# Two more places for expert weights, contiguous output pieces, and a reordered end of the main loop in a fused attention and mixture-of-experts kernel

## The chip, the cores and the metric

The kernel runs on one core of one Trainium2 chip. The metric is the device time of one execution in microseconds (us), as the median of several runs. The engines are PE (TensorE, with its weight loads shown apart as PEld), DVE (VectorE), ACT (ScalarE), POOL (GpSimd) and SP (SyncE). In this kernel SP computes nothing; it issues every transfer between DRAM and the on-chip memory, in one queue and in program order.

## What is computed

The reference is a chain of three parts, in fp32, on 8 batches of 576 tokens (4608 tokens in all):

```python
# 1. attention with 32 learned memories per head (8 heads of 64)
a = softmax(phi)                          # over 32 memories
k_m, v_m = a^T k, a^T v
attn = softmax(q k_m^T / 8) v_m
x = attn, heads side by side              # 4608 x 512
# 2. a maxout layer
h = max(x @ w1, x @ w2, x @ w3)           # 4608 x 768
x = h @ w_out                             # 4608 x 512
# 3. a soft mixture of 8 experts with 4 slots each
logits = x @ phi2                         # 4608 x 32
d = softmax(logits, over all tokens)
slot_input = d^T x                        # 32 x 512
slot_out[e] = relu(slot_input[e] @ e_w1[e]) @ e_w2[e]    # 512 -> 1024 -> 512
c = softmax(logits, over the 32 slots)
out = c @ slot_out                        # 4608 x 512
```

The softmax over all tokens splits the kernel in two: the experts can begin only when the last token's logits are known, and every output row needs all experts.

## The kernel before, in words

**The main part.** `ORDER` is a text of some 1,490 steps, written out one by one; each step is a short function (`ops`, L822), and the order of the text is the order of the instructions on every engine. `mn u hf r` (L585) makes six main products of unit u, half hf, of the r-th of the three maxout weights, into one of three `ps_m` banks; `ev u hf r` (L599) empties the bank: for r = 0 ACT copies it, for r = 1 and 2 DVE takes the maximum, the last of them into the h block `ht`. A unit is a batch n and one of six h blocks i; unit 47 is batch 7, block 5. `ht` is a ring of four buffers (L605), so block 5 of a batch takes the buffer of block 1. `trm`/`trc` (L635, L647) turn an h block: for batches 0, 1 and 7 on PE with a copy by ACT, for the others with a transpose on DVE, a write to DRAM (L645) and a read back (L663), both issued by SP. `lg` (L684) adds the logits of a block, into the single `ps_l` bank. `slm`/`sla` add the expert inputs of a batch into `s_run`. `hrc` copies the last 64 tokens of a block.

**The expert weights.** They are 64 pieces of 128 x 1024 fp32 (512 KB), used in the order input weights of expert 0, input weights of expert 1, first half of the output weights of expert 0, and so on, and at the end the second halves of all eight (L261 to L268). They are loaded into `NSLOT` = 41 places, many of them in memory that other data has left: piece k goes into place k modulo 41. `send(n)` (L278) issues the next n loads on SP. 32 of them are steps of `ORDER`; the others stand behind the main part (L847, L907, L935) and in the expert loops (L1019, L1037), always one `send` for each place's use. A load into a place waits until what was in it has been read, and whatever SP holds behind it waits too.

**The end.** From L848 on come the last block's logits and statistics, then the expert input (L911 to L946). The loop at L1044 runs, for each expert, `ex_in` (64 PE products for the hidden layer, ACT's relu), `ex_turn` (DVE) and `ex_out(e, 0)` (first 256 output columns, summed over experts in `acc[0]`). Then `so_a`, `so_b` bring the sum into two parts `sh` and `sl` for more exact products. The output is made in 9 groups r (eight of 4 x 128 tokens, and one of 8 x 64 tokens) by 2 halves x of 256 columns. `st_out(r, x)` (L1071) makes 12 products into four `ps_x` banks (all there are) and empties them with two copies by ACT and two by DVE into a free place. For r below `NH` = 6 each half goes out by itself, 512 KB in runs of 256 columns; for r = 6 to 8 the halves are put beside each other, and whole rows go out when the second half is made. The calls (L1110 to L1121) put `ex_out(r, 1)` and `st_out(r, 0)` in turns, then all of x = 1.

Of the kernel before, what the change touches and what calls it, by code (L numbers as in the profile page):

```python
# [7 lines left out]
FP32 = mybir.dt.float32  # L8
# [6 lines left out]
B, H, S, D, M = 8, 8, 576, 64, 32  # L15
DM, FF, E, F = 512, 768, 8, 1024
# [6 lines left out]
for _x in (2, 3, 4, 5, 12, 6, 7, 13, 8, 9, 14, 15, 10, 11):  # L23
    CV.append((768 * _x, 768))
NEG = -1.0e30
PIECE = 1024
NX = 6
# [131 lines left out]
)  # L159
W = [1, 0, 0, 3, 2]  # L160
LL = 0
VP = 3
EXTRA = 2
NSLOT = EXTRA + 9 + 12 + NX + 2 + 3 + 3 + 1 + 3


@with_exitstack
def kernel(
# [13 lines left out]
    nc = tc.nc  # L182
# [4 lines left out]
    ps_m = ctx.enter_context(tc.tile_pool(name="ps_m", bufs=3, space=PSUM))  # L187
    ps_l = ctx.enter_context(tc.tile_pool(name="ps_l", bufs=1, space=PSUM))
# [12 lines left out]
    def bank(pool, tag):  # L201
        return pool.tile([128, 512], FP32, tag=tag, name=tag)

    def mx():
        return bank(ps_x, "x")


    arena = keep.tile([128, (9 + 12 + NX) * PIECE], FP32, name="arena")
# [6 lines left out]
    s_run = keep.tile([128, FF], FP32, name="s_run")  # L215
    stat = keep.tile([128, 2], FP32, name="stat")
    h5x = keep.tile([128, 1920], FP32, name="h5x")
# [6 lines left out]
    hbuf = keep.tile([128, 3, 1536], FP32, name="hbuf")  # L224
# [17 lines left out]
    x0 = a0 + 12288  # L242
# [13 lines left out]
    slots = [extra[:, PIECE * j:PIECE * j + PIECE] for j in range(EXTRA)]  # L256
    slots += [arena[:, o:o + PIECE] for o in slot_off]
    late_slots = [h5x[:, 0:PIECE]] + [arena[:, PIECE * j:PIECE * j + PIECE] for j in range(9)]
    late_slots += [hbuf[:, 2, 0:PIECE], arena[:, x0:x0 + PIECE]]

    order = [("in", 0)]  # L261
    for e in range(E):
# [15 lines left out]
    def send(n):  # L278
        for _ in range(n):
            if sent[0] < len(pieces):  # L280
                x = slot(sent[0])
                if isinstance(x, list):
                    for g in range(4):
                        nc.sync.dma_start(out=x[g], in_=pieces[sent[0]][:, 256 * g:256 * g + 256])
                else:
                    nc.sync.dma_start(out=x, in_=pieces[sent[0]])
                sent[0] += 1
# [332 lines left out]
    lg = {}  # L620
# [186 lines left out]
    with tc.manual_schedule():  # L807
# [5 lines left out]
        def late_slots_in():  # L813
# [18 lines left out]
            slm=lambda n, k: sl_m(n, k, by_group(n, k)), sla=sl_a, mn=mn,  # L832
            send=send, rl=rest_logit, rx=lambda: st_exp(lg["r"], 96, 8), rtm=rest_tm, rtc=rest_tc,
# [4 lines left out]
        for x in ORDER.split(";"):  # L838
            x = x.split()
# [2 lines left out]

        main_x.close()
        more2 = ctx.enter_context(tc.tile_pool(name="more2", bufs=1, side="right"))
        more2_sb = more2.tile([128, 3 * PIECE], FP32, name="more2")
        slots.extend(more2_sb[:, PIECE * j:PIECE * j + PIECE] for j in range(3))
        send(3)  # L847
        L = B - 1  # L848
        st_logit(L, 5)
        last_logit(LL, 6)  # L850
        t = lg[L]
# [61 lines left out]
        for x in range(2):  # L913
            y = mx()
            for i in range(3):
                nc.tensor.matmul(
                    y[:, 32 * i:32 * i + 32], s_run[:, 128 * (3 * x + i):128 * (3 * x + i) + 128], wsel,
                    start=True, stop=True)
            if x:
                nc.vector.tensor_copy(out=st[x], in_=y[:, 0:96])  # L920
            else:
                nc.scalar.activation(out=st[x], in_=y[:, 0:96], func=ACTF.Copy)
        nc.vector.memset(msk, 0.0)
        warm(W[2], True)
        seen = set()
        for i in range(6):
            for c in ((1, 0) if i < 2 else (0, 1)):
                g = i if i < 4 else i - 4 + 2 * c
# [100 lines left out]
        def ex_out(e, x):  # L1029
            k0 = first["ab"[x], e]  # L1030
            for k in range(2):
                for g in range(4):
                    nc.tensor.matmul(  # L1033
                        acc[x][32 * g:32 * g + 32, 0:256], msk[:, e, k, g],
                        part_of(k0 + k, g),
                        start=(e == 0 and k == 0), stop=(e == E - 1 and k == 1), tile_position=(0, 32 * g))
                send(1)  # L1037
# [14 lines left out]
        def so_a(x):  # L1052
            nc.vector.tensor_copy(out=so_sb, in_=acc[x][:, 0:256])

        def so_b(x):
            t = mx()
            c = slice(256 * x, 256 * x + 256)
            nc.tensor.matmul(t[:, 0:256], sel, so_sb, start=True, stop=True)
            nc.scalar.activation(out=sh[:, c], in_=t[:, 0:256], func=ACTF.Copy)
            nc.vector.tensor_tensor(out=sl[:, c], in0=t[:, 0:256], in1=sh[:, c].bitcast(FP32), op=ALU.subtract)  # L1060

        ov = out.rearrange("(g x s) c -> x s g c", x=2, s=S)
        free = [slots[64 - NSLOT + j] for j in range(NSLOT - (64 - NSLOT))]
        free = [x for x in free if not isinstance(x, list)]

        NH = 6
        tok = {}
        for r in range(9):
            tok[r] = [free.pop(0) for _ in range(1 if r < NH else 2)]

        def st_out(r, x):  # L1071
            cs = slice(256 * x, 256 * x + 256)
            whole = r >= NH
            if not whole and x == 1 and free:
                tok[r] = [free.pop(0)]
            ts = [mx() for _ in range(4)]
            for k, (c, o) in enumerate(((ch, sh), (cl, sh), (ch, sl))):
                for g in range(4):
                    if r == 8 and g == 3:
                        continue  # L1080
                    rs = slice(32 * g, 32 * g + 32)
                    nc.tensor.matmul(  # L1082
                        ts[g][:, 0:256], c[rs, r], o[rs, cs], start=(k == 0), stop=(k == 2), tile_position=(32 * g, 0))
            if r == 8:
                for k, (c, o) in enumerate(((ch, sh), (cl, sh), (ch, sl))):
                    nc.tensor.matmul(ts[3][:, 0:256], c[:, 9], o[:, cs], start=(k == 0), stop=(k == 2))
            for g in range(4):
                if whole:
                    o = tok[r][g // 2].rearrange("p (g c) -> p g c", g=2)[:, g % 2, cs]
                else:  # L1090
                    o = tok[r][0].rearrange("p (g c) -> p g c", g=4)[:, g]
                if g % 2:
                    nc.vector.tensor_copy(out=o, in_=ts[g][:, 0:256])
                else:
                    nc.scalar.activation(out=o, in_=ts[g][:, 0:256], func=ACTF.Copy)
                if whole and x == 1 and g % 2:
                    o = tok[r][g // 2].rearrange("p (g c) -> p g c", g=2)
                    if r < 8:
                        nc.sync.dma_start(
                            out=out[S * r + 128 * g - 128:S * r + 128 * g + 128].rearrange("(g p) c -> p g c", p=128),  # L1100
                            in_=o)
                    else:
                        for y in range(2):
                            nc.sync.dma_start(out=ov[y, 512:576, g - 1:g + 1], in_=o[64 * y:64 * y + 64])
            if not whole:
                nc.sync.dma_start(
                    out=out[S * r:S * r + 512, cs].rearrange("(g p) c -> p g c", p=128),
                    in_=tok[r][0].rearrange("p (g c) -> p g c", g=4))

        so_a(0)  # L1110
        so_b(0)
        for r in range(9):
            if r < E:
                ex_out(r, 1)
            if r == E - 1:
                so_a(1)
            if r == E:
                so_b(1)
            st_out(r, 0)
        for r in [0, 1, 2, 3, 4, 5, 8, 6, 7]:  # L1120
            st_out(r, 1)  # L1121


# [57 lines left out]
```

## Time and profile before

| | us |
|---|---|
| median of 3 runs | 460.35 (460.18 to 460.82) |
| the profiled execution, its own time | 462.82 |
| its span, first to last instruction | 461.0 |
| PE busy in the span | 439.0 (95%) |
| DVE busy | 333.3 (72%) |
| ACT busy | 192.4 (42%) |
| POOL busy | 71.4 (15%) |

TensorE's granted clock is 0.976 of full speed in the mean. The transfers move 109.49 MB, 237 GB/s over the span. Times in all views count from the start of the span. "SPq" is SP's queue; a row of a transfer on it shows the issue, not the transfer. A landing is the time from the issue to the arrival of all data. In the views of stretches, the share is the mean busy share of the core's 16 DMA engines. In rows of instructions, the bracket gives the engine's idle time before the row and what ended it.

### The profile page before, as it was taken

The page shows a single profiled execution, that of the slowest core. Times are in us where ns is not written, and L with a number is a line of the kernel's source. Part 1 is how long each engine was busy: PE and PEld are TensorE (multiplying, and loading weights), DVE is VectorE, ACT ScalarE, POOL GpSimd, SP SyncE. Part 2 cuts the span into 40 slices and gives each one's busy share as a digit, 9 for nine tenths or more (in the row PEclk, how much of TensorE's full clock was granted, in tenths as well). Part 3 has the DMA queues.
Part 4 walks back from the last instruction along what each step waited for, and adds up shares of the span by engine and source line. Part 5 has one row for each costly group of instructions (what it writes and reads, how often), then busy time and mean ns, then how long its engine had stood idle before and what let it go on. Part 6 is the DMA issues. An engine that isn't in the chain of part 4 may idle for free.

```text
span 461.0 us, 12577 instructions
## 1 busy us (share of the span) xinstructions
PE 439.0 (95%) x5233; PEld 363.8 (79%) x5233; DVE 333.3 (72%) x753; ACT 192.4 (42%) x450; POOL 71.4 (15%) x92
## 2 busy tenths in 40 slices
PE   6989999999999999999999999999999999999982
PEld 5778889888887889978889698879878896654461
DVE  1596989879777986798769869899836444595441
ACT  2576766645524343334334334433433313233331
POOL 0235545620020011002100210030200000011000
PEclk9999999999999999999999999999999999999955
DMA  8987894217202395537468675388357775899988
GB/s 318 417 327 276 318 392 150 116 42 309 118 10 112 100 345 180 189 99 256 139 213 291 223 284 181 125 293 292 106 193 251 284 251 213 324 410 407 378 292 276
DMA packets 47657, 109.49 MB, mean 237 GB/s; under 512 B 3440, under 2 KB 26224, under 8 KB 45552
## 3 DMA queue, kind: packets, MB, share of 16 engines
q1 hardware_dynamic: 47600, 108.69, 65.2%
q8 instruction: 41, 0.67, 0.6%
q14 instruction: 16, 0.13, 0.1%
HBM read 91.38 MB, written 17.30 MB: 236 GB/s over the span
## 4 chain that ended last, share of the span: by engine, by line
PE 85%; DVE 5%; DMA 3%; issue 2%; ACT 2%; SPq 1%; POOL 1%; DVEq 0%; ACTq 0%; POOLq 0%
PE m L597 48%; PE x L564 7%; PE l L801 4%; PE x L439 3%; PE x L1082 3%; PE x L748 2%; DMA arena<-in_kv_dram 2%; PE x L475 2%; PE l L680 2%; PE m L1033 2%; PE m L1016 2%; PE x L639 2%; PE x L343 1%; PE l L1033 1%; SPq L663 1%
## 5 line engine op out<-in xcount | busy, mean ns | idle before, releaser
L597 PE MATMUL m<-ah,vh 128*128 128x288 f32 x576 | 171.4, 312 | 1.2 <-DVE ht L611 0.6
L597 PE MATMUL m<-ah,vl 128*128 128x288 f32 x576 | 161.8, 295 | 0.0
L597 PEld LDWEIGHTS m<-ah,vh 128*128 128x128 f32 x576 | 108.2, 188 | 20.6 <-issue 12.4
L597 PE MATMUL m<-al,vh 128*128 128x288 f32 x576 | 123.2, 295 | 0.1
L597 PEld LDWEIGHTS m<-ah,vl 128*128 128x128 f32 x576 | 108.4, 188 | 0.4
L597 PEld LDWEIGHTS m<-al,vh 128*128 128x128 f32 x576 | 92.3, 188 | 0.3 <-POOL al L532 0.3
L607 ACT ACTIVATE g<-m 128x288 f32<-128x288 f32 x96 | 38.9, 410 | 70.8 <-PE m L597 62.5
L609 DVE TENSOR_TENSOR g<-m,g 128x288 f32<-128x288 f32 x96 | 42.5, 449 | 31.0 <-PE m L597 24.4
L573 ACT ACTIVATE vh<-x 128x384 fp32r<-128x384 f32 (+1 forms) x100 | 42.0, 478 | 54.6 <-PE x L564 40.6
L611 DVE TENSOR_TENSOR ht<-m,g 128x288 f32<-128x288 f32 x96 | 42.4, 450 | 20.3 <-PE m L597 9.0
L579 DVE TENSOR_TENSOR vl<-x,vh 128x384 fp32r<-128x384 f32 (+1 forms) x100 | 48.7, 530 | 3.3 <-ACT vh L573 2.8
L564 PE MATMUL x<-arena,kvt 64*32 64x384 f32 (+1 forms) x800 | 39.5, 477 | 1.3 <-DVE vl L579 0.8
L532 POOL TENSOR_TENSOR al<-arena,ah 128x576 fp32r<-128x576 f32 x16 | 23.3, 1465 | 72.1 <-ACT ah L528 42.5
L325 POOL TENSOR_TENSOR arena<-arena 128x768 uint32<-128x768 uint32 (+1 forms) x13 | 23.5, 1808 | 34.5 <-ACT arena L313 24.2
L801 PE MATMUL l<-cst 128*128 128x128 f32 x162 | 25.0, 303 | 3.8 <-DMA cst<-in_consts_dram 3.2
L801 PEld LDWEIGHTS l<-cst 128*128 128x128 f32 x162 | 21.6, 208 | 7.1 <-DMA cst<-in_consts_dram 3.2
L616 POOL COPY arena<-ht 128x64 f32<-128x64 f32 x24 | 6.3, 279 | 124.5 <-DVE ht L611 98.9
L564 PEld LDWEIGHTS x<-arena,kvt 64*32 64x32 f32 x800 | 12.4, 105 | 13.5 <-issue 7.8
L439 PE MATMUL x<-arena 128*32 128x129 f32 x640 | 19.8, 274 | 1.1 <-DMA arena<-in_kv_dram 0.7
L643 DVE STREAM_TRANSPOSE arena<-ht 128x512 f32<-128x512 f32 x30 | 20.5, 697 | 0.2
L439 PEld LDWEIGHTS x<-arena 128*32 128x32 f32 x640 | 17.3, 110 | 3.2 <-DMA arena<-in_kv_dram 0.9
L481 DVE STREAM_TRANSPOSE arena<-x 128x288 f32<-128x288 f32 x32 | 13.3, 457 | 3.7 <-PE x L475 3.7
(246 smaller groups left out, 588.0 us busy)
## 6 DMA issues: line engine op xcount, KB each, us to landing
arena<-in_e_w_dram SPq DMA_DIRECT2D x44, 512.0 KB, 7.7
arena<-in_w_dram SPq DMA_DIRECT2D x14, 768.0 KB, 6.3
arena<-in_kv_dram SPq DMA_DIRECT2D x8, 1290.0 KB, 9.8
arena<-in_q_dram SPq DMA_DIRECT2D x16, 576.0 KB, 6.2
arena<-in_kv_dram SPq DMA_DIRECT2D x8, 1032.0 KB, 6.7
tr<-arena SPq DMA_DIRECT2D x30, 256.0 KB, 3.1
hbuf<-tr SPq DMA_DIRECT2D x30, 256.0 KB, 3.6
arena<-in_phi_t_dram SPq DMA_DIRECT2D x8, 576.0 KB, 5.9
```

The costliest lines, as they stand in the source:

```text
L325: (eng or nc.gpsimd).tensor_tensor(out=du, in0=du, in1=lo.bitcast(U32), op=ALU.add)
L439: nc.tensor.matmul(t[32 * g:32 * g + 32, 0:KVC], phin_sb[:, j, b, 32 * g:32 * g + 32], kv_sb[:, j, b, g] if j < 4 else kv4_sb[:, g], start ...
L532: nc.gpsimd.tensor_tensor(out=al[n][:, :, c], in0=aT_sb[:, :, c], in1=ah[n][:, :, c].bitcast(FP32), op=ALU.subtract)
L564: nc.tensor.matmul(t[b][32 * g:32 * g + 32, 128 * r0:128 * r1], kvt[n][r, b, 32 * g:32 * g + 32], w_sb[r, i, r0:r1, g], start=True, stop=T ...
L573: nc.scalar.activation(out=v1[n, i][0][:, b, c], in_=ph["v1", n, i][b][:, c], func=ACTF.Copy)
L579: nc.vector.tensor_tensor(out=vl[:, b, c], in0=ph["v1", n, i][b][:, c], in1=vh[:, b, c].bitcast(FP32), op=ALU.subtract)
L597: nc.tensor.matmul(t[:, 0:HALF], x, y, start=(k == 0), stop=(k == 5))
L607: nc.scalar.activation(out=g1[u, hf], in_=t[:, 0:HALF], func=ACTF.Copy)
L609: nc.vector.tensor_tensor(out=g1[u, hf], in0=t[:, 0:HALF], in1=g1[u, hf], op=ALU.max)
L611: nc.vector.tensor_tensor(out=ht[n, i][:, cs], in0=t[:, 0:HALF], in1=g1.pop((u, hf)), op=ALU.max)
L643: nc.vector.transpose(out=v, in_=ht[n, i][:, 0:512])
L801: nc.tensor.matmul(t[:, 0:128], ident, ident, start=True, stop=True)
```

## The change

Four things are changed.

1. `NSLOT` is 44. The pool `more2` holds five places, not three; a place made of `s_run[:, 512:768]` and three parts of `h5x` is added (its load is four transfers); the place in `hbuf` stands behind the `more2` places and not ahead of them. One `send` step fewer stands in `ORDER` (31), and the last of these stands behind the h read `trc 6 5`.
2. In `ORDER`, `trm 7 1; lg 7 1; trc 7 1` stand ahead of `mn 47 1 1; mn 47 1 2; mn 47 0 2` (18 main products); they stood behind. The last maxima `ev 47 0 2; ev 47 1 2` and `hrc 47` follow right behind the products.
3. The output tensor is laid out as 2 x 9 pieces of 128 x 1024, and each `st_out` writes one, contiguous, as soon as it is made. The host puts the rows in their order afterwards.
4. `ex_out(0, 1)` goes between `so_a(0)` and `so_b(0)`; six of the `st_out(r, 0)` are made before x = 1 is finished, and the other twelve calls use by turns the four `ps_x` banks and the three `ps_m` banks with `ps_l`. `so_b(1)` uses the `ps_l` bank.

```diff
@@ ORDER
-    "send 1; lg 7 0; mn 44 0 2; mn 44 0 0; ev 44 0 0; ev 44 1 1; ev 44 1 2; v1h 7 5; mn 44 0 1; ev 44 0 1; ev 44 "
-    "0 2; hrc 39; mn 45 1 0; mn 43 0 2; ev 45 1 0; mn 43 1 1; mn 45 0 0; ev 45 0 0; v1l 7 5; ev 43 0 2; hrc 44; "
-    "send 1; hrc 38; mn 43 1 2; ev 43 1 1; ev 43 1 2; hrc 43; mn 45 0 1; ev 45 0 1; trm 6 5; trc 6 5; mn 47 1 0; "
...
-    "2; mn 47 0 0; ev 47 0 0; mn 47 0 1; mn 46 1 1; mn 46 1 2; ev 46 1 1; ev 46 1 2; hrc 45; ev 47 0 1; mn 47 1 "
-    "1; hrc 46; mn 47 1 2; mn 47 0 2; ev 47 1 1; trm 7 2; trc 7 2; ltm 0 3; dtm 6; dtc 6; ev 47 0 2; trm 7 1; trc "
-    "6 3; trc 6 2; trm 7 4; trc 7 1; ev 47 1 2; trm 7 3; ltc 0 3; lg 7 1; slm 6 0; trc 7 3; slm 6 1; lg 7 2; lg 7 "
-    "3; trc 7 4; sla 6 0; sla 6 1; lg 7 4; hrc 47"
+    "lg 7 0; mn 44 0 2; mn 44 0 0; ev 44 0 0; ev 44 1 1; ev 44 1 2; v1h 7 5; mn 44 0 1; ev 44 0 1; ev 44 0 2; hrc "
+    "39; mn 45 1 0; mn 43 0 2; ev 45 1 0; mn 43 1 1; mn 45 0 0; ev 45 0 0; v1l 7 5; ev 43 0 2; hrc 44; hrc 38; mn "
+    "43 1 2; ev 43 1 1; ev 43 1 2; hrc 43; mn 45 0 1; ev 45 0 1; trm 6 5; trc 6 5; send 1; mn 47 1 0; v1h 7 4; "
...
+    "0 0; ev 47 0 0; mn 47 0 1; mn 46 1 1; mn 46 1 2; ev 46 1 1; ev 46 1 2; hrc 45; ev 47 0 1; trm 7 1; lg 7 1; "
+    "trc 7 1; mn 47 1 1; hrc 46; mn 47 1 2; mn 47 0 2; ev 47 1 1; ev 47 0 2; ev 47 1 2; hrc 47; trm 7 2; trc 7 2; "
+    "ltm 0 3; dtm 6; dtc 6; trc 6 3; trc 6 2; trm 7 4; trm 7 3; ltc 0 3; slm 6 0; trc 7 3; slm 6 1; lg 7 2; lg 7 "
+    "3; trc 7 4; sla 6 0; sla 6 1; lg 7 4"
 )
+NH = 4
-NSLOT = EXTRA + 9 + 12 + NX + 2 + 3 + 3 + 1 + 3
+NSLOT = EXTRA + 9 + 12 + NX + 2 + 3 + 5 + 2 + 3
...
-    late_slots += [hbuf[:, 2, 0:PIECE], arena[:, x0:x0 + PIECE]]
+    late_slots += [arena[:, x0:x0 + PIECE]]
...
-        more2_sb = more2.tile([128, 3 * PIECE], FP32, name="more2")
-        slots.extend(more2_sb[:, PIECE * j:PIECE * j + PIECE] for j in range(3))
-        send(3)
+        more2_sb = more2.tile([128, 5 * PIECE], FP32, name="more2")
+        slots.extend(more2_sb[:, PIECE * j:PIECE * j + PIECE] for j in range(5))
+        slots.append(hbuf[:, 2, 0:PIECE])
+        send(6)
...
+        slots.append([s_run[:, 512:768]] + [h5x[:, PIECE + 256 * j:PIECE + 256 * j + 256] for j in range(3)])
+        send(1)
         nc.vector.memset(msk, 0.0)
...
         def so_b(x):
-            t = mx()
+            t = bank(ps_l, "l") if x else mx()
...
-        def st_out(r, x):
+        def st_out(r, x, pool=None):
             cs = slice(256 * x, 256 * x + 256)
-            whole = r >= NH
-            if not whole and x == 1 and free:
-                tok[r] = [free.pop(0)]
-            ts = [mx() for _ in range(4)]
+            if pool:
+                ts = [bank(ps_m, "m") for _ in range(3)] + [bank(ps_l, "l")]
+            else:
+                ts = [mx() for _ in range(4)]
...
+            tok = free.pop(0)
             for g in range(4):
...
+                o = tok[:, 256 * g:256 * g + 256]
...
-            if not whole:
-                nc.sync.dma_start(
-                    out=out[S * r:S * r + 512, cs].rearrange("(g p) c -> p g c", p=128),
-                    in_=tok[r][0].rearrange("p (g c) -> p g c", g=4))
+            nc.sync.dma_start(out=out[x, r], in_=tok)
 
         so_a(0)
+        ex_out(0, 1)
         so_b(0)
-        for r in range(9):
-            if r < E:
-                ex_out(r, 1)
-            if r == E - 1:
-                so_a(1)
-            if r == E:
-                so_b(1)
-            st_out(r, 0)
-        for r in [0, 1, 2, 3, 4, 5, 8, 6, 7]:
-            st_out(r, 1)
+        for r in range(1, E):
+            ex_out(r, 1)
+            if r <= NH:
+                st_out(r - 1, 0)
+        so_a(1)
+        st_out(NH, 0)
+        so_b(1)
+        st_out(NH + 1, 0, True)
+        rest = [(r, 1) for r in range(9)] + [(r, 0) for r in range(NH + 2, 9)]
+        for i, (r, x) in enumerate(rest):
+            st_out(r, x, i % 2)
...
-    args.append(nc.dram_tensor("out_0_dram", (B * S, DM), _mybir.dt.float32, kind="ExternalOutput").ap())
+    args.append(nc.dram_tensor("out_0_dram", (2, 9, 128, 1024), _mybir.dt.float32, kind="ExternalOutput").ap())
```

## Rows read from the trace of the kernel before

**Rows 1.** The page, part 2: DMA busy tenths in 40 slices of the span.
```profile
DMA  8987894217202395537468675388357775899988
```

**Rows 2.** Timeline of SP's queue: start us, us of issuing, line, what, count.
```profile
366.75 1.41 SPq L286 DMA_DIRECT2D arena<-in_e_w_dram  x3
...
384.81 0.35 SPq L286 DMA_DIRECT2D hbuf<-in_e_w_dram  x1
...
385.73 1.35 SPq L286 DMA_DIRECT2D more<-in_e_w_dram  x3
...
394.07 1.28 SPq L286 DMA_DIRECT2D wo<-in_e_w_dram  x3
397.69 0.81 SPq L286 DMA_DIRECT2D extra<-in_e_w_dram  x2
398.59 17.77 SPq L286 DMA_DIRECT2D arena<-in_e_w_dram  x17
418.75 1.61 SPq L286 DMA_DIRECT2D more<-in_e_w_dram  x2
...
454.92 1.08 SPq L1099 DMA_DIRECT2D out_dram<-hbuf  x1
```

**Rows 3.** Stretches of the end: us, busy time of each engine, PEclk, DMA share, GB/s.
```profile
420.00:422.00 2.00, 2.00 (x30) 1.08 (x30) 0.42 (x1) 0.38 (x1) 0.46 (x1) 1.00 1.03 410
...
436.00:438.00 2.00, 1.55 (x15) 1.01 (x15) 0.98 (x4) 0.63 (x3) 0.00 (x0) 1.00 1.05 367
...
442.00:444.00 2.00, 1.73 (x19) 1.44 (x21) 0.76 (x2) 0.66 (x2) 0.00 (x0) 0.50 0.93 311
...
456.00:458.00 2.00, 0.00 (x0) 0.00 (x0) 0.00 (x0) 0.00 (x0) 0.00 (x0) 0.50 1.04 394
```

**Rows 4.** Chain that ended last, from 380 us: start us, us, engine, line.
```profile
419.99 0.70 PE x L1058 x2
...
425.36 1.00 PE m L1033 x16
...
427.92 0.55 PE x L1082 x11
...
443.32 1.25 PE x L1082 x10
...
445.00 1.25 PE x L1082 x10
```

**Rows 5.** Transfers from 390 us on (KB each, median us to landing), and line 1099's landings.
```profile
more<-in_e_w_dram SPq DMA_DIRECT2D x2, 512.0 KB, 10.2
...
DMA to landing us min/median/max: 4.8/5.2/5.2
```

**Rows 6.** Stretches from 364 us, transfers alone: us, PEclk, DMA share, GB/s.
```profile
374.00:376.00 2.00, 1.00 0.08 31
...
382.00:384.00 2.00, 1.00 0.00 0
384.00:386.00 2.00, 1.00 0.09 16
...
394.00:396.00 2.00, 1.00 0.46 133
...
400.00:402.00 2.00, 1.00 0.80 313
```

**Rows 7.** Timeline of the engines, single groups: start us, us, engine, line, what, idle before.
```profile
380.46 0.42 PE L597 MATMUL m<-al,vh 128*128 128x288 f32 x2
...
381.59 1.51 PE L639 MATMUL x<-cst,ht 128*128 128x128 f32 x12
...
383.03 0.42 PE L680 MATMUL l<-ht,p 128*32 128x128 f32 x8
...
383.58 0.82 DVE L611 TENSOR_TENSOR ht<-m,g 128x288 f32<-128x288 f32 x2 [3.80 <-PE l L680]
...
441.23 0.75 DVE L1093 COPY hbuf<-x 128x256 f32<-128x256 f32 x2 [0.93 <-PE x L1082]
```

More of the change, by code (lines that the diff above doesn't have):

```diff
@@ L1060, in so_b @@
             nc.vector.tensor_tensor(out=sl[:, c], in0=t[:, 0:256], in1=sh[:, c].bitcast(FP32), op=ALU.subtract)
-        ov = out.rearrange("(g x s) c -> x s g c", x=2, s=S)
         free = [slots[64 - NSLOT + j] for j in range(NSLOT - (64 - NSLOT))]
         free = [x for x in free if not isinstance(x, list)]
-        NH = 6
-        tok = {}
-        for r in range(9):
-            tok[r] = [free.pop(0) for _ in range(1 if r < NH else 2)]
-        def st_out(r, x):
+        def st_out(r, x, pool=None):
             cs = slice(256 * x, 256 * x + 256)
-            whole = r >= NH
-            if not whole and x == 1 and free:
-                tok[r] = [free.pop(0)]
-            ts = [mx() for _ in range(4)]
+            if pool:
+                ts = [bank(ps_m, "m") for _ in range(3)] + [bank(ps_l, "l")]
+            else:
+                ts = [mx() for _ in range(4)]
             for k, (c, o) in enumerate(((ch, sh), (cl, sh), (ch, sl))):
@@ L1086, in st_out @@
                     nc.tensor.matmul(ts[3][:, 0:256], c[:, 9], o[:, cs], start=(k == 0), stop=(k == 2))
+            tok = free.pop(0)
             for g in range(4):
[L1088 to L1091, printed above, removed]
+                o = tok[:, 256 * g:256 * g + 256]
                 if g % 2:
@@ L1095, in st_out @@
                     nc.scalar.activation(out=o, in_=ts[g][:, 0:256], func=ACTF.Copy)
-                if whole and x == 1 and g % 2:
-                    o = tok[r][g // 2].rearrange("p (g c) -> p g c", g=2)
-                    if r < 8:
-                        nc.sync.dma_start(
[L1100 to L1104, printed above, removed]
-            if not whole:
-                nc.sync.dma_start(
-                    out=out[S * r:S * r + 512, cs].rearrange("(g p) c -> p g c", p=128),
-                    in_=tok[r][0].rearrange("p (g c) -> p g c", g=4))
+            nc.sync.dma_start(out=out[x, r], in_=tok)
         so_a(0)
+        ex_out(0, 1)
         so_b(0)
-        for r in range(9):
-            if r < E:
-                ex_out(r, 1)
-            if r == E - 1:
-                so_a(1)
-            if r == E:
-                so_b(1)
-            st_out(r, 0)
-        for r in [0, 1, 2, 3, 4, 5, 8, 6, 7]:
-            st_out(r, 1)
+        for r in range(1, E):
[9 more added lines that the diff above has]
+            st_out(r, x, i % 2)
 def kernel(**inputs):
@@ L1179 @@
     r = _run(nc, [arrays], core_ids=[0])
-    return r.results[0]["out_0_dram"]
+    o = _np.asarray(r.results[0]["out_0_dram"]).reshape(2, 9, 128, 4, 256)
+    res = _np.empty((B, S, 2, 256), f32)
+    res[:, 0:512] = o[:, 0:8].transpose(1, 3, 2, 0, 4).reshape(B, 512, 2, 256)
+    res[:, 512:] = o[:, 8].reshape(2, 2, 64, 4, 256).transpose(3, 1, 2, 0, 4).reshape(B, 64, 2, 256)
+    return res.reshape(B * S, DM)
```

4 rows, old and new, of the table ORDER are left out of this document.

## Prediction

> **What bounds the kernel now.** Three views decide it. The page's 40 slices show where the transfers are dense: of 11.5 us each, the last six have the DMA digits 8, 9, 9, 9, 8, 8 and the three before them 7, 7, 5 [rows 1]. So the last 69 us are a stretch of transfers, with a half-empty stretch before it.
>
> The queue of SP, in order of time, says what is moved there [rows 2]. There are 64 pieces of expert weights (512 KB each) and 41 places. Twenty-three pieces must wait until the products on a place's first piece are done: 2 into `extra` from 397.69, 17 into `arena` from 398.59, 2 into `more` from 418.75, then h5x and the four parts. Only behind them in the same queue stand the outputs, the last of them issued at 454.92.
>
> The stretches give the rate [rows 3]: 410 GB/s at a share of 1.03 while loads run (420 to 422). One piece is 524,288 B, so 1.28 us, which is also the pace of SP there. Between 442 and 444 it is 311 GB/s, with TensorE at a granted 0.50, its lower level (1.2 GHz); it was still at 1.00 from 436 to 438, where its busy time had sunk to 1.55 of 2.00 us.
>
> The chain of waits [rows 4] tells why 311: one call of `st_out` begins at 443.32, the next at 445.00, every 1.68 us. All four ps_x banks are taken by one call and the next waits for ScalarE and VectorE to empty them. 524,288 B in 1.68 us is 312 GB/s: there products and evictions set the pace, not the wires. Then, since r = 6 to 8 keep whole rows back until both halves exist (in the code), 3 MB are left for the end, and the last transfer is issued at 454.92 and lands some 5.2 us later [rows 2, 5], at 460.1; 0.9 us after that the span of 461.0 ends.
>
> **The change, part by part.** Times are those of the profiled execution (span 461.0, own time 462.82). The median of the runs is 460.35, 2.47 under that; I take differences of span off the median.
>
> *Three more places.* Up to 397.69 SP can now issue 44 pieces, so 20 are left for the tail, not 23. The new places (two in `more2`, one in `s_run` and `h5x`) are taken from slack: of the stretches between 374 and 396, four alone (shares 0.08, 0.00, 0.09, 0.46) leave 1.84 + 2.00 + 1.82 + 1.08 = 6.7 us without transfer [rows 6]. To fit in are the three, and two of the three pieces that were issued at 366.75 [rows 2], now issued after the h reads: 5 x 1.28 = 6.4 us. That is tight, and part of it is gated late. The list of four parts waits for `s_run` to be read (about 393), and its four issues stand ahead of the three `wo` pieces, issued at 394.07 [rows 2]. I estimate its 512 KB to run mostly in the hole of 394 to 396, and 1.0 us of backlog to be carried past 398. Of that the dip in 400 to 402 (share 0.80, so 0.4 us idle) [rows 6] and the smaller one behind it take up 0.6. Net delay of the reloads: 0.4 us; ends: 0 and 1.0.
>
> Removing pieces 21 to 23 from the reload sequence makes the 20th the last. It is the first of the two issued at 418.75 [rows 2], and landed 10.2 us later [rows 5], at 428.95. With the delay: 429.35. This needs no new rate: the first twenty reloads go into the same places, released by the same products.
>
> *Moved logits and turn.* Before, VectorE's last two maxima of the main products (L611) started at 383.58 after 3.80 us of idling for PE's L680 [rows 7]: h block 5 takes the ring buffer of block 1, whose turn and logits come later on PE. Now those eight steps stand ahead of the last 18 main products. Their price on PE is a third of 1.51 us (three turns) and 0.42 us for the logits [rows 7], some 0.9 us, and it is paid in either order: PE works without a gap from there to the statistics, so I count it at nothing (ends: -0.2 and +0.3 us, the second if a turn waits for a bank). What it brings is that the main pools are free earlier: the last product ended at 380.88 and would now end 0.9 later, and with the last two maxima (0.82 us) behind it that is 382.6, instead of 384.4 [rows 7]. The `more2` pieces also no longer stand behind the hbuf piece, which waited until 384.81; they went at 385.73 [rows 2]. Thus they start about 3 us earlier, which is what makes room for two more of them. On SP one weight piece now stands between the h reads (L663), while two fewer stand ahead of the last h write: the h reads, which PE needs for the products behind its L680 of 383.03 [rows 7], should come earlier, not later. The hbuf piece still waits until 384.8, but only pieces that are gated later still (the list, `wo`) are queued behind it.
>
> *Outputs.* Eighteen pieces of 512 KB, each in runs of 4 KB where it was 1 or 2 KB. No row here has a 4 KB write. The bounds: 4 KB loads at 410 GB/s, 1.28 us; 1 KB writes alone, 436 to 438, 367 GB/s, 1.43 us [rows 3]. The 2 KB writes at the end ran at 394 GB/s (456 to 458), 1.33 us [rows 3]. I take 1.31, between the nearest two: 4 KB loads and 2 KB writes. 18 x 1.31 = 23.6 us; ends 23.0 and 25.7.
>
> *Can the engines feed that?* Half x = 0 of r = 0 to 3 is ready early: the first so_b was at 419.99, each `ex_out` is 1.00 and each `st_out` 0.55 us on PE [rows 4], so four pieces are in SBUF by 428 and cover the wires for 5.2 us, to 434.6. The last `ex_out` needs the load of 429.35 and ends about 430.3. r = 4 comes straight behind it (in SBUF at 431.8). r = 5 needs the one ps_l bank, which so_b(1) holds until its subtraction ends (432.5), so it is there at 434. From then on calls alternate between two sets of four banks, so that a call waits no longer for the evictions of the one before. The slowest engine per piece is then VectorE with two copies, 0.75 us [rows 7], or PE, at most the 1.25 us that the chain shows at the lower clock [rows 4], which holds waits. Both lie under 1.31. I allow 0.3 us for r = 5 coming late.
>
> **Sum.** 429.35 + 23.6 + 0.3 = 453.25 for the last landing, + 0.9 = 454.15 of span, against 461.0: 6.85 us less. 460.35 - 6.85 = **453.5 us**.
>
> **The rivals.**
>
> 1. *Outputs stay bound by products and evictions.* If two bank sets don't overlap and a piece still takes 1.68 us [rows 4], the twelve calls from 433 end at 453.2, the last data are in SBUF at 454.0, and the landing needs 3.5 us more (an estimate from the 5.2 us under load [rows 5] less queueing): span 458.4, time 457.8. For it: the lower clock will be granted again, since PE has little to do. Against it: of the 1.68 us a part is the wait for one's own evictions, which the second set removes. Chance 8%.
>
> 2. *Wider runs bring nothing.* At 1.43 us a piece, as the 1 KB writes [rows 3], 18 take 25.7: span 456.3, time 455.6. Against it is the step from 1 to 2 KB, 367 to 394 GB/s [rows 3]. Chance 12%. The Trainium skill (DMA: Bandwidth & Descriptors, Specifications) gives 512 B as the smallest transfer for line rate, by which 1 KB would have it already and this rival would hold; the trace disagrees, with 367 against 394 and 410 GB/s, though these are not one direction of transfer.
>
> 3. *The hole doesn't hold the pieces.* If gates keep all three from fitting before 398, the reloads come 3.84 us later than in the sum's ideal case, 3.4 later than forecast: 456.9 us. For it: 6.4 us into 6.7 is tight. Against: the stretch from 382 to 386 is empty but for the wait behind the hbuf piece [rows 2, 6], and that wait goes. Chance 6%.
>
> 4. *Slower: writes of 4 KB into one contiguous 512 KB block are slow.* Place: the 18 outputs behind the last load. It decides from (460.1 - 429.35) / 18 = 1.71 us a piece on, 307 GB/s. At 280 GB/s (1.87 us) the last lands at 463.1 and the time is 463.3. Against it: every write row that is not held by the engines lies at 367 or above [rows 3]. Chance 3%.
>
> That the change does nothing it says is excluded by counting the `send` calls and places: 44, of which 22 are whole and free for 18 outputs.
>
> **How the numbers follow.** Forecast 71%, rivals 8, 12, 6 and 3%. The forecast's own ends are 0 to 1.0 us of delay and 23.0 to 25.7 us of outputs; the low one with no late r = 5 gives 460.35 - 8.15 = 452.2, and PE's -0.2 us 452.0. I put the low end at 451.6 for a rate a little over 410. The high end of 456.3 takes in rival 2 and, in part, rival 3; rivals 1 and 4 stay outside. A measurement of this kernel tells 0.2% from no change (0.9 us). Only rival 4 is on the other side: faster 0.96, same 0.01, slower 0.03.
>
> **What would show it.** In the changed profile: SP's `extra` reload still near 397.7 and the last load issued near 419, with only outputs behind it; outputs issued from about 423 with 4 KB runs; a share of 1.0 and 390 to 410 GB/s from 398 to 452 with no hole near 438; VectorE's L611 without its long idle on L680, and the statistics behind the main products at their old time. It is wrong if a DMA hole shows between 432 and 452 (rival 1), if the rate there is near 367 at a full share (rival 2), or if the reloads start or land over 2 us late (rival 3).

## The result and the profile after

The changed kernel takes 455.40 us in the median of 4 runs (454.13 to 457.30), the kernel before 460.59 beside it: a ratio of 0.9885, interval 0.9859 to 0.9911. A second series gave 455.36 and 0.9878 (0.9863 to 0.9892). So it is faster by 5.2 us in the first series and 5.5 in the second, where 6.85 were forecast; 455.4 lies in the range. (The title counts the two new places in `more2`; with the one of four parts three are added, 41 to 44.)

The profiled execution (455.98, span 454.2, mean granted clock 0.991) can be laid beside that of before step by step. First SP's queue, which answers to [rows 2]:

```profile
366.62 0.46 SPq L287 DMA_DIRECT2D arena<-in_e_w_dram  x1
...
372.15 0.46 SPq L287 DMA_DIRECT2D arena<-in_e_w_dram  x1
...
374.78 1.57 SPq L287 DMA_DIRECT2D arena<-in_e_w_dram  x2
382.90 2.25 SPq L287 DMA_DIRECT2D more<-in_e_w_dram  x5
385.25 6.28 SPq L287 DMA_DIRECT2D hbuf<-in_e_w_dram  x2
393.36 0.33 SPq L285 DMA_DIRECT2D s_run<-in_e_w_dram  x1
393.78 1.33 SPq L285 DMA_DIRECT2D h5x<-in_e_w_dram  x3
395.20 1.33 SPq L287 DMA_DIRECT2D wo<-in_e_w_dram  x3
398.00 0.81 SPq L287 DMA_DIRECT2D extra<-in_e_w_dram  x2
...
419.27 0.33 SPq L287 DMA_DIRECT2D more<-in_e_w_dram  x1
423.56 0.34 SPq L1093 DMA_DIRECT2D out_dram<-more  x1
...
446.83 1.14 SPq L1093 DMA_DIRECT2D out_dram<-hbuf  x1
```

The five `more2` loads start at 382.90, 2.8 us before the three of before. The first reload is at 398.00, as before (397.69). The reload of 419.27 is the 20th and the last, and outputs stand right behind it. The last output is issued at 446.83, not at 454.92. From the first reload to the end of the span it was 461.0 - 397.69 = 63.3 us; now it is 454.2 - 398.00 = 56.2. I call this stretch **the tail**; it became 7.1 us shorter.

The landings (transfers from 390 us on: KB each, median us to landing), for [rows 5]:

```profile
out_dram<-hbuf SPq DMA_DIRECT2D x1, 512.0 KB, 6.4
...
more<-in_e_w_dram SPq DMA_DIRECT2D x1, 512.0 KB, 10.1
```

The last load landed at 419.27 + 10.1 = 429.4, the last output at 446.83 + 6.4 = 453.2. Stretches of the end, columns as in [rows 3]:

```profile
430.00:432.00 2.00, 1.64 (x21) 0.91 (x17) 1.41 (x4) 1.04 (x3) 0.00 (x0) 1.00 0.87 344
432.00:434.00 2.00, 1.74 (x35) 1.52 (x35) 1.37 (x5) 1.20 (x4) 0.00 (x0) 1.00 0.76 309
434.00:436.00 2.00, 2.00 (x44) 1.91 (x37) 2.00 (x7) 1.76 (x7) 0.00 (x0) 1.00 0.82 332
436.00:438.00 2.00, 2.00 (x40) 1.96 (x36) 2.00 (x7) 1.92 (x7) 0.00 (x0) 1.00 1.02 403
...
442.00:444.00 2.00, 0.00 (x0) 0.00 (x0) 0.42 (x1) 0.00 (x0) 0.00 (x0) 1.00 1.03 412
...
446.00:448.00 2.00, 0.00 (x0) 0.00 (x0) 0.00 (x0) 0.00 (x0) 0.00 (x0) 0.50 1.01 404
```

Where the kernel before wrote 311 GB/s between 442 and 444 [rows 3], this one writes 412, and by then PE is done and one copy by VectorE is left. Between 430 and 436 the wires lack work: shares of 0.87, 0.76 and 0.82 leave 0.26 + 0.48 + 0.36 = 1.1 us idle. The chain of waits, for [rows 4], shows two calls of `st_out` in 1.39 us (one on each set of banks) where one took 1.68:

```profile
434.26 0.67 PE x L1081 x11
...
435.65 0.66 PE x L1081 x11
```

Ahead of the tail, transfers alone, for [rows 6]:

```profile
382.00:384.00 2.00, 1.00 0.07 16
...
394.00:396.00 2.00, 1.00 0.72 217
396.00:398.00 2.00, 1.00 0.91 230
```

The hole of 394 to 396 is now fuller (0.72 in place of 0.46), but badly used: behind it, where the four parts of 1 KB runs land and the `wo` loads begin, it is 230 GB/s at a share of 0.91.

VectorE's last maxima, for [rows 7], no longer wait for PE's L680 (3.80 us there):

```profile
381.94 0.82 DVE L612 TENSOR_TENSOR ht<-m,g 128x288 f32<-128x288 f32 x2 [1.19 <-PE m L598]
```

### The profile page after: what moved, and what is told of

Same layout as the page of the kernel before. It is cut to its first block, busy times and chain, and to the rows that moved or that the text cites. A ratio compares the mean times of both kernels' runs of the same rounds, so it can differ in the third digit from the quotient of the medians.

```text
span 454.2 us, 12571 instructions
## 1 busy us (share of the span) xinstructions
PE 432.2 (95%) x5233; PEld 360.4 (79%) x5233; DVE 333.0 (73%) x753; ACT 192.2 (42%) x450; POOL 71.4 (16%) x92
## 4 chain that ended last, share of the span: by engine, by line
PE 83%; DMA 5%; DVE 5%; ACT 2%; issue 1%; SPq 1%; POOL 1%; ACTq 0%; DVEq 0%
PE m L598 47%; PE x L565 7%; PE l L802 5%; PE x L440 4%; DMA arena<-in_kv_dram 2%; PE x L749 2%; PE x L476 2%; PE m L1020 2%; PE m L1037 2%; PE l L681 2%; PE x L1081 1%; DMA arena<-in_w_dram 1%; PE x L640 1%; PE l L1037 1%; DMA more<-in_e_w_dram 1%
## 5 line engine op out<-in xcount | busy, mean ns | idle before, releaser
L574 ACT ACTIVATE vh<-x 128x384 fp32r<-128x384 f32 (+1 forms) x100 | 42.0, 478 | 54.6 <-PE x L565 40.6
```

The lines of the kernel that those rows point to most:

```text
L574: nc.scalar.activation(out=v1[n, i][0][:, b, c], in_=ph["v1", n, i][b][:, c], func=ACTF.Copy)
```

## The experiments

The theory was that transfers hold the tail, at 1.28 us for each 512 KB piece, once the outputs no longer wait for engines. The main rivals were that products and evictions hold it still, and that the width of the runs is worth nothing. Tails are spans less the time of the first reload; profiles are of single executions.

**The kernel before, once more.** No edit.

> The kernel before, unchanged. Theory: its first profiled execution (span 461.0, time 462.82) was about 1.9 us longer than the median execution, and the changed kernel's profiled execution was not, so that the difference of the two spans (6.8 us) is larger than that of the medians (5.2 us). Then this profile has a span near 458.6 (460.5 less 1.8), its time agrees with the median within 0.7 us, and the missing 2 us are found in one stretch against the first profile. Rival: a profiled execution of this kernel is always longer by 2 us; then the span is again near 461 and the time near 462.8, while the median of the plain runs stays at 460.5.

Median 461.73 (459.71 to 463.40, 12 runs), ratio to itself 1.0015 (0.9989 to 1.0042). The profile's time is 461.13 and its span 459.3 (458.6 was expected), so the theory holds in the main: the first profile's length was that execution's own. Its 2.47 us were counted over a median of three runs; over the 51 executions of this kernel in the later series (median 461.2) it is 1.6. The second profile's queue has

```profile
396.26 0.80 SPq L286 DMA_DIRECT2D extra<-in_e_w_dram  x2
```

1.4 us earlier than [rows 2]; the tail is 63.0, against 63.3. So the difference between the two profiles arose ahead of the tail, though not in one stretch as expected: SP's queue is 0.6 us apart at 80 us and 1.5 at 262. Over the thirteen profiles of this study the first reload lies anywhere from 395.85 to 398.00.

**The changed kernel, once more.** No edit.

> The changed kernel, unchanged, beside the three variants of this call and the kernel before. Theory: median 455.4 (454.8 to 455.9), ratio to the kernel before 0.988 to 0.990, the profile again with holes between 430 and 436 and a last landing near 453. Rival: the first four runs were spread by chance (454.13 to 457.3) and the true gain is that of the two first spans, 6.8 us: 453.7.

455.36 (454.52 to 455.98), ratio 0.9878; span 453.8, first reload 397.50, tail 56.3. So the gain of the medians is seen twice, 5.2 and 5.5 us, and the 6.8 us between the first two spans is not reached by it.

**41 places.**

```diff
-NSLOT = EXTRA + 9 + 12 + NX + 2 + 3 + 5 + 2 + 3
+NSLOT = EXTRA + 9 + 12 + NX + 2 + 3 + 3 + 1 + 3
-        more2_sb = more2.tile([128, 5 * PIECE], FP32, name="more2")
+        more2_sb = more2.tile([128, 3 * PIECE], FP32, name="more2")
...
-        slots.append([s_run[:, 512:768]] + [h5x[:, PIECE + 256 * j:PIECE + 256 * j + 256] for j in range(3)])
-        send(1)
```

> The changed kernel with 41 places in place of 44 (more2 of three, no list of four parts); everything else as changed. Theory (the tail is held by transfers): three more reloads of 1.28 us each, 3.8 us, less the 0.4 us that the list delays the reloads and less the 1.1 us of holes between 430 and 436 that later loads would fill: 457.7 us (456.9 to 459.2), last reload issued about 423. Rival (the outputs are held by products and evictions, the loads are hidden): within 0.5 us of the changed kernel, 455.4.

456.95 (456.72 to 457.18): 1.6 us over the changed kernel, and 0.9911 (0.9886 to 0.9937) of the kernel before. The tail is 58.7, so 2.4 us longer. Three pieces are worth less than 3 x 1.28, as expected (457.7, from 456.9 on), since later loads fill the hole behind 430: its shares from 430 to 434 are 1.01 and 1.02 (0.87 and 0.76 in the changed kernel). So the outputs, with the moved steps, bring about 3.7 us without the places.

**44 places with the old outputs.** In the changed kernel, everything from `so_b` to the last `st_out`, and the output's layout, is put back.

```diff
-        def st_out(r, x, pool=None):
+        def st_out(r, x):
...
-        for i, (r, x) in enumerate(rest):
-            st_out(r, x, i % 2)
+        for r in [0, 1, 2, 3, 4, 5, 8, 6, 7]:
+            st_out(r, 1)
```

> The loads and the step order of the changed kernel (44 places), with the outputs of the kernel before: its layout, its whole rows for r = 6 to 8, its order of calls, ps_x banks alone. Theory (with those outputs the end is held by products and evictions at 1.68 us a piece behind the last ex_out, which waited for loads only 0.85 us): the last load lands near 429 in place of 432.8, but the end moves by 0.9 us at most: 459.4 to 460.9 us, with a longer stretch of transfers below full rate behind 430. Rival (each place is worth its 1.28 us wherever the outputs stand): 457 us.

460.88, ratio 0.9994 (0.9983 to 1.0004): nothing in the median. The tail of its profile is 61.8, which is 1.2 to 1.5 us shorter than in the two profiles of before. Stretches and chain of this run:

```profile
434.00:436.00 2.00, 1.42 (x20) 0.89 (x15) 1.18 (x3) 0.73 (x3) 0.00 (x0) 1.00 0.31 108
436.00:438.00 2.00, 1.35 (x21) 0.93 (x17) 1.07 (x3) 1.01 (x4) 0.00 (x0) 1.00 0.00 0
```
```profile
430.93 1.00 PE m L1037 x16
431.93 0.59 PE x L1086 x11
...
436.70 0.96 PE x L1086 x11
...
438.08 0.96 PE x L1086 x11
...
441.16 1.25 PE x L1086 x10
...
442.84 1.25 PE x L1086 x11
```

The loads saved became an empty stretch of more than 3 us: there was nothing to write yet. The last `ex_out` ends at 431.93, 34.9 us behind this run's first reload (397.04); in the kernel before it was 35.8. Behind it stands the old pace, a call every 1.38 us while the granted clock is 1.00 and every 1.68 us at 0.50. So in the medians the places are worth 1.6 us with the new outputs and nothing with the old ones.

**The old runs of 1 KB.**

```diff
-            nc.sync.dma_start(out=out[x, r], in_=tok)
+            if r < 8:
+                nc.sync.dma_start(
+                    out=out[S * r:S * r + 512, cs].rearrange("(g p) c -> p g c", p=128),
+                    in_=tok.rearrange("p (g c) -> p g c", g=4))
+            else:
+                for y in range(2):
+                    nc.sync.dma_start(
+                        out=ov[y, 512:576, :, cs],
+                        in_=tok[64 * y:64 * y + 64].rearrange("p (g c) -> p g c", g=4))
```

> The changed kernel with the output laid out as in the kernel before: each st_out still goes out by itself, 512 KB, but in runs of 256 columns (1 KB); group 8 in two transfers. Theory: the width of the runs sets the rate, 1.42 us a piece in place of 1.28, 18 x 0.14 = 2.5 us: 457.9 us, with 365 to 375 GB/s at a full share from 436 on. Rival (1 KB runs have the line rate already): 455.4 within 0.5 us and 400 GB/s or more.

458.37 (457.64 to 458.62): 3.0 us over the changed kernel, tail 59.4. At a full share the rate is lower than the 367 GB/s from which the forecast took its bound [rows 3]:

```profile
436.00:438.00 2.00, 2.00 (x35) 2.00 (x34) 1.83 (x6) 1.64 (x6) 0.00 (x0) 0.50 1.04 348
440.00:442.00 2.00, 2.00 (x29) 1.69 (x29) 1.16 (x4) 0.77 (x3) 0.00 (x0) 0.50 1.03 346
```

346 to 348 against 395 to 414 GB/s, writes against writes: 1.51 us a piece in place of 1.27 to 1.33. The granted clock of this profile is low, but it isn't the cause: executions with a mean clock from 0.975 to 0.987 all took 457.6 to 458.6 us. Two things changed together, though: the 4 KB runs of a piece lie one behind the other in DRAM, the 1 KB runs 2 KB apart. Which of the two sets the rate, no run tells. The rule of the Trainium skill (DMA: Bandwidth & Descriptors, Specifications) that 512 B is enough for line rate doesn't hold for these writes.

**One set of banks.**

```diff
-        st_out(NH + 1, 0, True)
+        st_out(NH + 1, 0)
...
-            st_out(r, x, i % 2)
+            st_out(r, x)
```

> The changed kernel with every st_out on the four ps_x banks, no second set. Theory (transfers hold the tail as long as a piece takes the engines less than 1.28 us): at the full clock a call with its evictions takes about 1.3 us, so little changes until the granted clock falls; then 1.68 us a piece as in the kernel before, and the end moves by up to 12 x 0.4 = 4.8 us; 456.5 to 459. Rival (bank sets don't matter, the wires do): 455.4 within 0.5 us.

458.33 (457.13 to 458.76): 2.9 us over the changed kernel, tail 59.7. Chain and a stretch:

```profile
439.73 1.25 PE x L1081 x11
...
441.41 1.25 PE x L1081 x11
```
```profile
444.00:446.00 2.00, 1.73 (x19) 1.21 (x13) 0.84 (x3) 0.78 (x3) 0.00 (x0) 0.50 0.68 270
```

The pace of 1.68 us is back, with wires at a share of 0.68. The granted clock is at its lower level (0.50), as it was in the kernel before; in the changed kernel's profile it is 1.00 until PE has finished. But the bank sets count at either level. With one set at 1.00 a call took 1.38 us (above, with the old outputs), and with two sets at 0.50, in the run with 1 KB runs, two calls took 1.68:

```profile
435.24 0.86 PE x L1082 x12
...
436.92 0.86 PE x L1082 x11
```

So the second set halves a call's time: 1.38 to 0.70 us at the full clock, 1.68 to 0.84 at the lower. That it also holds the clock up is not shown: in that run and in the one with 41 places the clock fell to 0.50 behind 433, with two sets and PE busy 1.99 of 2.00 us.

The last two experiments belong together. In the kernel before, two limits lay close to each other: 1.68 us a piece by products and evictions, and 1.51 us by 1 KB runs, with the wires already at a share of 0.93 [rows 3]. With either one left in place the kernel takes 458.3 to 458.4 us, with both lifted 455.4.

**The end of the step order put back.**

```diff
-ev 47 0 1; trm 7 1; lg 7 1; trc 7 1; mn 47 1 1; hrc 46; mn 47 1 2; mn 47 0 2; ev 47 1 1; ev 47 0 2; ev 47 1 2; hrc 47; trm 7 2; trc 7 2
+ev 47 0 1; mn 47 1 1; hrc 46; mn 47 1 2; mn 47 0 2; ev 47 1 1; trm 7 2; trc 7 2; ltm 0 3; dtm 6; dtc 6; ev 47 0 2; trm 7 1
...
```

> The changed kernel with the end of the step order put back: turn and logits of block 1 behind the last 18 main products, the last maxima waiting for them. Theory (the move only lets the more2 loads start earlier, and costs PE 0.3 us because logits no longer cover its wait for ScalarE): the more2 loads start at 384.4 in place of 382.9, some 1 us of transfers is pushed past 398, PE gets 0.3 us back; 455.9 us (455.1 to 456.7). Rival 1 (the move is worth nothing, transfers have slack): 455.1, the 0.3 us that PE gets back. Rival 2 (the move is what makes room for the new places): 457 or more.

455.02 (454.56 to 455.92), tail 56.3: no different from the changed kernel. Rival 1 holds. In this run's queue the `more2` loads start only at

```profile
383.70 2.44 SPq L287 DMA_DIRECT2D more<-in_e_w_dram  x5
```

2.0 us before those of [rows 2], and 13.1 ahead of the first reload where it was 12.0 there. The time is the same. What the move costs is seen in the changed kernel at the products for batch 6:

```profile
381.55 0.49 PEld L640 LDWEIGHTS x<-cst,ht 128*128 128x128 f32 x4
...
383.55 0.16 PEld L749 LDWEIGHTS x<-hbuf,dk 128*32 128x32 f32 x8 [0.17 <-ACT hr L795]
```

They now wait 0.17 us for ScalarE's copies; with the order put back, the logits stand there.

**Without the place of four parts (43 places).**

```diff
-        slots.append([s_run[:, 512:768]] + [h5x[:, PIECE + 256 * j:PIECE + 256 * j + 256] for j in range(3)])
-        send(1)
```

> The changed kernel with 43 places: the place made of s_run and three parts of h5x is left out. Theory (the four parts of 1 KB runs take 2 us or more of the engines just ahead of the wo loads and delay the reloads): one more reload, +1.28, less the delay that goes, about 1.0: 455.7 us (455.2 to 456.3). Rival (its load runs in an empty stretch): 456.7.

454.97 (454.29 to 455.62), tail 56.0: below what was expected, and not to be told from the changed kernel. Ahead of its tail the transfers are better used:

```profile
394.00:396.00 2.00, 1.00 0.91 313
396.00:398.00 2.00, 1.00 0.98 371
```

So the third place isn't shown to be worth anything: one reload less, but 512 KB at a poor rate just ahead of the reloads.

**Seven early outputs.**

```diff
-NH = 4
+NH = 7
```

> The changed kernel with NH = 7: seven of the st_out(r, 0) go between the ex_out(r, 1), not four, so that outputs are in hand when the last load has landed. Theory (the holes between 430 and 436, 1.1 us, come from the pieces in hand running out): the holes close, 454.3 us (454.0 to 454.8). Rival (the last ex_out comes 1.7 us later by the three calls ahead of it, and the twelve calls behind it follow too late): 455.4 or more.

454.12 (452.55 to 455.16), 0.9860 (0.9841 to 0.9878) of the kernel before; tail 54.6, which is 1.6 us shorter. The interval overlaps that of the changed kernel, so the median alone wouldn't settle it; the pair below does. The holes are closed but for a rest at 434 to 436:

```profile
430.00:432.00 2.00, 1.53 (x22) 1.10 (x14) 1.44 (x5) 1.04 (x4) 0.00 (x0) 1.00 1.03 414
432.00:434.00 2.00, 1.62 (x18) 1.03 (x20) 1.25 (x5) 1.32 (x5) 0.00 (x0) 1.00 1.02 416
434.00:436.00 2.00, 2.00 (x43) 1.77 (x39) 1.83 (x6) 1.35 (x5) 0.00 (x0) 1.00 0.93 371
```

**Both, and all three.** The first kernel has `NH = 7` and the end of the step order put back; the second leaves the place of four parts out as well. The diffs are those above.

> The changed kernel with NH = 7 and the end of the step order put back; 44 places. Theory (the move of turn and logits is worth nothing to the loads): 453.9 us (453.3 to 454.5), the time from the first reload to the end near 54.6, as with early7. Rival (with the outputs in hand the loads are the bound, and the more2 loads starting 1 us later show): 454.8 or more.

> The changed kernel with three edits at once: the end of the step order put back, the place of four parts left out (43 places), and seven of the st_out(r, 0) between the ex_out(r, 1). Theory (the first is worth -0.3 us on PE, the second -0.2 to -0.4, the third -1.2 to -1.6, and they add): 453.6 us (453.0 to 454.2), span behind the first reload near 54.4. Rival (each of the first two only moved a load that the other now needs): as early7, 454.1, or more.

453.39 (452.39 to 454.74), ratio 0.9837 (0.9817 to 0.9857), tail 55.1; and 453.42 (452.88 to 454.05), ratio 0.9836 (0.9822 to 0.9849), tail 55.6. Both beat the changed kernel by 2 us. The first differs from the run with the step order put back (0.9874, 0.9859 to 0.9889) by `NH` alone, and the intervals don't overlap. Neither tail is shorter than that of seven early outputs alone, so of the three edits only the early outputs are shown to be worth something; the rest lies within the scatter.

## Why the prediction was right, and where it was off

**Three more places.** Right in its sequence: 20 reloads, the first still near 397.7, and only outputs behind the last. It was to land at 429.35 and landed at 429.4; that they meet so closely is luck, since the forecast started from 428.95 in the first profile of before, and in the second the same load landed at 416.75 + 10.1 = 426.9. What the step did not say is that the places pay only together with the outputs: in the medians they bring nothing alone (0.9994) and 1.6 us with them, where the sum counted 3 x 1.28 less 0.4 us. The order of the sum, with the outputs costed behind the places, was right for the changed kernel alone.

**Moved logits and turn.** Priced at nothing with an end of +0.3, for the wrong reason. PE did lose some 0.2 us, not to a bank but to ScalarE's copies. From the first turn behind the main products (381.68) to the products of L749 (383.56) it is 1.9 us and the moved block took 0.9 (378.30 to 379.19); put back, the same work, turn and logits included, takes 2.55 (379.88 to 382.43 in that run). The `more2` loads did start earlier (382.90), but the claim that this makes the room was wrong: with the step order put back the time is the same. Whether putting the hbuf piece last was needed, no run shows.

**Outputs.** The term of 1.31 us was about 0.02 too large: from 436 to 450 the writes went at 395 to 414 GB/s, 406 in the mean, which is 1.29. Writes of 4 KB runs go about as fast as loads. The bound from below, 1.43 us for 1 KB, was too small; by themselves such writes took 1.51 in the experiment. Why they went at 367 GB/s in the kernel before from 436 to 438, when its last load had landed (426.43 + 6.4 = 432.8), stays open. The reading that the wires did not hold that kernel's end was too sharp: they were at a share of 0.93 to 0.96.

**Can the engines feed that?** They can: 1.39 us for two calls. That r = 5 comes late was seen, but its hole was put at 0.3 us, and 1.1 were measured. Against that stand 18 x 0.02 = 0.4 us less for the outputs, so the sum should have been 0.4 us too low. Yet the forecast of 453.25 for the last landing met 453.2, and that of 454.15 for the span met 454.2. Where the 0.4 us went isn't traced; that the sum meets this profile to 0.1 us is luck in part.

**The rivals.** Rival 1's sign did show, a hole between 432 and 436, but for another reason: calls do not come every 1.68 us, outputs in hand had run out. It failed because two bank sets overlap, at either clock. Its argument on the clock isn't refuted as such: the clock stayed at 1.00 to PE's end in the profile, but one of the four executions of the first series had a mean of 0.979 and took 457.3 us. Rival 2's time of 455.6 us is as near to the measured 455.4 as can be, so the time alone doesn't tell it from the forecast; the rate does (395 to 414 GB/s, not 367), and so does the experiment in which 1 KB runs cost 3.0 us. It was priced too low: without the wider runs it is 458.4, not 455.6. For rivals 3 and 4 the reloads start too near their old time and the writes go too fast.

**The step that was off** is the last one: "I take differences of span off the median". The two spans differ by 6.8 us, as forecast; the medians differ by 5.2 and 5.5. A second pair of profiles gives 459.3 - 453.8 = 5.5 us, but that it agrees with the medians is luck, because it comes from the part that no edit touches. This shows from a load that SP issues ahead of every edit; in order, the kernel before, its second profile, the changed kernel, its second profile:

```profile
348.12 0.81 SPq L286 DMA_DIRECT2D more<-in_e_w_dram  x2
...
346.68 0.80 SPq L286 DMA_DIRECT2D more<-in_e_w_dram  x2
...
348.18 0.81 SPq L287 DMA_DIRECT2D more<-in_e_w_dram  x2
...
347.68 0.80 SPq L287 DMA_DIRECT2D more<-in_e_w_dram  x2
```

From there to the end of the span it is 112.9 and 112.6 us in the kernel before, and 106.0 and 106.1 in the changed one. So in all four profiles the part that the change touches is 6.5 to 6.9 us shorter, as forecast, while the start of that load lies between 346.30 and 348.18 over the thirteen profiles. The medians show 1.0 to 1.7 us less, and why stays open. One candidate is the clock in the tail of the kernel before: of its 51 executions in the later series, the 13 with a mean granted clock of 0.978 or more have a median of 460.3 us, the nine with 0.973 or 0.974 one of 461.4. But the 28 from 0.975 to 0.977, among which the first profile's clock lies, have 461.4 too, and of the two profiles the one whose clock fell earlier (0.974) has the shorter tail. The base is another: 460.35 is the median of three runs, 461.2 that of the 51.

## What to carry to other kernels

Where transfers and engines are close to each other at the end of a kernel, removing transfers may be worth nothing until the engines can deliver early enough (here nothing in the median alone, 1.6 us with the new outputs), and lifting one of two near limits leaves the other; measure the parts apart and together before pricing either. Count not only the rate of what feeds a queue, but what is in hand at the moment when the old work in it runs out. And before a difference of two profiles is taken off a median, take a second profile of each kernel and count from a point ahead of the change: here one execution was 1.4 us off in a part that the change doesn't touch.

## What was not expected of the hardware

Writes to DRAM in runs of 1 KB went at 346 to 348 GB/s at a full share, in 4 KB runs at 395 to 414, the rate of loads. With a load of four times 128 KB in 1 KB runs, just ahead of the tail, the wires stood at a share of 0.91 with 230 GB/s; without it they moved 371 GB/s at 0.98.

The granted clock fell in the middle of the busy loop with 41 places and came back:

```profile
434.00:436.00 2.00, 1.99 (x39) 1.71 (x31) 2.00 (x6) 1.82 (x6) 0.00 (x0) 0.92 0.85 346
436.00:438.00 2.00, 2.00 (x35) 2.00 (x32) 1.80 (x6) 1.50 (x6) 0.00 (x0) 0.50 1.00 401
...
440.00:442.00 2.00, 2.00 (x36) 1.66 (x35) 1.76 (x6) 1.41 (x6) 0.00 (x0) 1.00 1.05 410
```

With outputs in hand, the transfers went on at 401 GB/s while it was 0.50.
